# Gated linear attention, soft mixture of experts and gated feed-forward on one core: the first six chunks prepared one at a time, three more w_out blocks converted earlier

## The chip, the cores and the metric

The kernel runs on one core of one Trainium2 chip. The core has five engines that run side by side and meet through semaphores: PE (matrix products, into PSUM), DVE (vector work), ACT (scalar functions and copies), POOL (a second, slower vector engine) and SP, which here only issues DMAs. The metric is the device time of one execution in microseconds (us). Before the change, three runs gave 400.57, 405.32 and 405.67 us; the median is 405.32 us. The profile is of one execution of 403.42 us, whose span from the first to the last instruction is 401.6 us.

## The reference

Three layers follow one another, all in float32 (the gate, value and output weights come as float64):

```python
# attention: 4 batches x 8 heads, 768 tokens, head size 48; the state is 48x48 per head
state = alpha[:, :, t, :, None] * state + einsum('bhd,bhe->bhde', k[:, :, t], v[:, :, t])
y[:, :, t] = einsum('bhd,bhde->bhe', q[:, :, t], state)
# soft mixture of experts: x is 3072 x 384, 8 experts with 4 slots each, hidden 1024
logits = x @ phi
d = softmax over tokens of logits;  c = softmax over slots of logits
slot_out[e] = maximum((d.T @ x)[e] @ w1[e], 0) @ w2[e]
x = c @ slot_out
# gated feed-forward: hidden 1536
xn = x / sqrt(mean(x * x) + 1e-6) * rms_g
out = (silu(xn @ w_gate) * (xn @ w_val)) @ w_out
```

## The kernel before

**Attention.** The 3072 tokens are 24 chunks of 128 tokens, six per batch. A chunk holds all eight heads as four pairs. Within a chunk the recurrence is turned into matrix products: running products of alpha (`R`, L449) and running inverse products from the chunk's other end (`iR`, L457 and L458) scale q and k, then PE makes the scores (L509), ACT moves them out of PSUM (L513), POOL clears what lies after the diagonal (L517), and PE multiplies with v (L530, L535) and with the state carried from the chunk before (L543, L547). DVE writes the next state (L553, op `sv`). The scalings are done for a *unit* of chunks at a time: units of 1, 2 and then 3 chunks, those of 2 and 3 in two halves (two pairs of heads each). One half is: load of alpha, k and q (L431), scans on DVE (L449, L457, L458), k multiplied on DVE and q multiplied on POOL (both L473). Alpha has two buffers, so the third load of alpha waits for the scans of the first.

**The other layers.** After every four chunks the logits, the running softmax over tokens and the slot sums are updated (function `group`). After the last chunk a short chain joins these (L680 to L692) and ends in `siT`, the slots' inputs (op `mi`, L692). The experts follow: 8 products with w1 (L749), each with a relu, a transpose and a product with w2 (L770); w1 and w2 come in 32 loads each (L734, L736) of 384 KB. Then the output side of the mixture is folded into the gate weights (L902 to L928), and the feed-forward runs 72 steps: two products (L1019), silu on ACT (L1054), a multiplication on DVE (L1056), a split into a high part on ACT (L1058) and a low part on DVE (L1061), and twelve products with w_out (L1026 to L1028).

**The float64 weights.** w_gate, w_val and w_out come in 36 pieces of 384 KB. Each is converted by five operations, in the function `wide_ops`: load `cl` (SP, L382), `ca` (ACT, L385 and L386), `cb` (DVE, L389 and L390), `cc` (POOL, L394) and `cd` (DVE, L397). A w_out block is then split into high and low parts (`hi` on ACT, L889, and `lo` mostly on POOL, L891). The first pieces are in the list `sooner`, of length `FIRST`: 15 pieces before the change, that is six gate and value pieces, w_out blocks 0 to 2, and six more gate and value pieces. `HOLD` says what a piece's `ca` waits for: nothing for the first nine, `mi` for those up to `FIRST`, and for pieces 15 to 17 (w_out blocks 3 to 5) `OHOLD`, the first low part of the feed-forward.

**What sets the order.** All operations of the program are entered in a plan with an engine, a cost, a priority, what they follow and which buffers they take. `Plan.times` simulates the engines and puts the operations in an order per engine; the instructions are issued in that order, and each engine and the DMA queue of SP work strictly in it. Besides fixed rings there are 58 blocks (ring `Q`) of 776 columns, of which the attention's buffers cover the first 24 until they are no longer used; weights, conversions and later intermediates take free blocks. A load that has no free block waits at the head of SP's queue, and the loads behind it wait too.

**Warm-up.** `WARM` groups of four transposes of a constant are entered with the lowest priority, so that the plan puts them where it expects PE to idle.

## Time and profile before

| | |
|---|---|
| runs | 400.57, 405.32, 405.67 us |
| profiled execution | 403.42 us, span 401.6 us |
| PE busy | 374.9 us (93%) |
| DVE busy | 299.0 us (74%) |
| ACT busy | 216.8 us (54%) |
| POOL busy | 122.6 us (31%) |
| DMA | 68.43 MB, 48.7% of 16 engines over the span |

The span falls into stages that differ in what limits them, so the shares over the whole span say little. The attention ends at 152.15 us, when the first expert product starts; the experts end at about 183 us; the feed-forward's first product with w_out starts at 194.63 us and the last ends at about 395 us. In a table by stage the columns are the stretch, its length, the busy time and count of each engine's instructions, the granted clock of TensorE (1.00 is 2.4 GHz, 0.50 is 1.2 GHz), the busy share of the 16 DMA engines, and GB/s. In a timeline a row is: start, time taken, engine, line, operation, what it writes and reads, count, and in square brackets the idle time of the engine ahead of it and what ended it.

### The profile page before, as it was taken

The numbers are of one execution on the slowest core, as the hardware profiler recorded it, in microseconds if no ns is written. First come the engines' busy times: TensorE is split into PE (matmuls) and PEld (weight loads), VectorE is DVE, ScalarE is ACT, GpSimd is POOL, SyncE is SP. The second block draws the span as 40 slices with busy tenths as digits, with TensorE's granted clock in tenths as the row PEclk, the third lists the DMA queues.
The fourth block names the chain that finished last, engine by engine and source line by source line (L and its number), as shares of the span: only waits on it lengthen the run. The fifth ranks groups of instructions, "written<-read, shape, count | busy, mean of one in ns | idle before, by whom it ended". The sixth has DMA issues, their size and how long they took to land.

```text
span 401.6 us, 8927 instructions
## 1 busy us (share of the span) xinstructions
PE 374.9 (93%) x3427; PEld 316.1 (79%) x3427; DVE 299.0 (74%) x563; ACT 216.8 (54%) x469; POOL 122.6 (31%) x150
## 2 busy tenths in 40 slices
PE   7689979998899999999889999999999999999993
PEld 6578858785777865436578999979899999999992
DVE  7999979879898557615989987769855667657652
ACT  2336535666574847311676786858856444444440
POOL 3445452635665415600155523243400000000000
PEclk9769989999999999999969999999999999999997
DMA  7899998996989679993021323213000102102012
GB/s 270 282 330 316 333 347 297 341 373 255 341 266 341 204 229 342 346 325 113 2 78 43 116 78 114 85 41 118 0 2 0 53 27 81 55 24 81 32 48 87
DMA packets 29252, 68.43 MB, mean 170 GB/s; under 512 B 3600, under 2 KB 9872, under 8 KB 29200
## 3 DMA queue, kind: packets, MB, share of 16 engines
q1 hardware_dynamic: 29200, 67.77, 48.7%
q8 instruction: 29, 0.48, 0.5%
q14 instruction: 23, 0.19, 0.1%
HBM read 63.04 MB, written 4.72 MB: 169 GB/s over the span
## 4 chain that ended last, share of the span: by engine, by line
PE 64%; DVE 16%; DMA 12%; issue 3%; ACT 2%; POOL 1%; SPq 0%; DVEq 0%; POOLq 0%; ACTq 0%
PE pstr L1019 4%; PE pssc L1019 4%; PE psmisc L1026 3%; PE pskn L1028 3%; PE psmisc L1028 3%; PE psy L1026 3%; PE psmisc L1027 3%; PE psU L1026 3%; PE pssc L509 3%; PE psy L1028 3%; PE psy L1027 3%; PE psU L1028 3%; PE psU L1027 3%; PE pskn L1026 3%; PE psy L530 3%
## 5 line engine op out<-in xcount | busy, mean ns | idle before, releaser
L1061 DVE TENSOR_TENSOR b<-b,b 128x512 fp32r<-128x512 f32 (+1 forms) x73 | 50.7, 697 | 26.3 <-PE psmisc L1027 10.1
L394 POOL TENSOR_TENSOR b<-b 128x384 int32<-128x384 int32 x36 | 40.5, 1126 | 96.5 <-DVE b L390 40.4
L1058 ACT CAST b<-b 128x512 fp32r<-128x512 f32 (+1 forms) x73 | 44.8, 617 | 36.6 <-DVE b L1056 34.5
L1056 DVE TENSOR_TENSOR b<-b,pssc 128x512 f32<-128x512 f32 (+1 forms) x73 | 49.2, 677 | 15.4 <-ACT b L1054 15.0
L1054 ACT ACTIVATE b<-pstr 128x512 f32<-128x512 f32 (+1 forms) x73 | 43.0, 594 | 24.2 <-PE pstr L1019 21.8
L517 POOL TENSOR_SCALAR_AFFINE_SELECT b<-b 128x512 f32<-128x512 f32 x48 | 32.2, 690 | 35.0 <-ACT b L513 34.9
L473 POOL TENSOR_TENSOR b<-b,b 128x768 f32<-128x768 f32 (+1 forms) x17 | 28.9, 1705 | 26.6 <-DVE pstr L457 12.2
L530 PE MATMUL psy<-b,b 128*48 128x128 f32 x384 | 29.7, 295 | 5.2 <-POOL b L517 4.3
L513 ACT COPY b<-pssc 128x512 f32<-128x512 f32 x48 | 26.7, 592 | 12.6 <-PE pssc L509 12.5
L458 DVE TENSOR_TENSOR_SCAN b<-b,pstr 128x387 f32<-128x387 f32 (+1 forms) x34 | 31.0, 912 | 1.7
L449 DVE TENSOR_TENSOR_SCAN b<-b,pstr 128x387 f32<-128x387 f32 (+1 forms) x34 | 29.0, 894 | 3.5 <-DMA b<-in_alpha_rows_dram 3.5
L509 PE MATMUL pssc<-b,b 48*128 48x128 f32 x384 | 30.1, 294 | 1.6 <-ACT b L513 1.2
L397 DVE SCALAR_TENSOR_TENSOR b<-b,b 128x384 int32<-128x384 int32 x36 | 27.2, 764 | 5.8 <-POOL b L394 5.8
L1019 PE MATMUL pssc<-y,b 128*128 128x512 f32 (+1 forms) x73 | 29.3, 401 | 2.1 <-DVE b L1056 1.7
L509 PEld LDWEIGHTS pssc<-b,b 48*128 48x128 f32 x384 | 24.8, 194 | 7.6 <-issue 4.9
L530 PEld LDWEIGHTS psy<-b,b 128*48 128x48 f32 x384 | 22.3, 131 | 10.5 <-POOL b L517 5.2
L1019 PE MATMUL pstr<-y,b 128*128 128x512 f32 (+1 forms) x73 | 29.4, 403 | 0.4 <-DVE b L906 0.4
L385 ACT ACTIVATE b<-b 128x384 f32<-128x384 f32 x36 | 20.8, 577 | 11.6 <-DMA b<-in_moe_w_val_dram 4.1
L1026 PE MATMUL pskn<-b,b 128*128 128x384 f32 x72 | 25.5, 354 | 0.2 <-ACT b L1058 0.2
L1028 PE MATMUL pskn<-b,b 128*128 128x384 f32 x72 | 24.9, 345 | 0.8 <-DVE b L1061 0.8
L1026 PE MATMUL psmisc<-b,b 128*128 128x384 f32 x72 | 24.7, 343 | 0.1
L1026 PE MATMUL psU<-b,b 128*128 128x384 f32 x72 | 24.6, 341 | 0.1
(226 smaller groups left out, 884.0 us busy)
## 6 DMA issues: line engine op xcount, KB each, us to landing
b<-in_moe_w_dram SPq DMA_DIRECT2D x64, 384.0 KB, 5.8
b<-in_alpha_rows_dram SPq DMA_DIRECT2D x14, 387.5 KB, 5.6
b<-in_k_rows_dram SPq DMA_DIRECT2D x14, 384.0 KB, 5.0
b<-in_q_rows_dram SPq DMA_DIRECT2D x14, 384.0 KB, 5.6
b<-in_v_rows_dram SPq DMA_DIRECT2D x24, 192.0 KB, 5.2
b<-in_moe_w_gate_dram SPq DMA_DIRECT2D x12, 384.0 KB, 4.8
b<-in_moe_w_val_dram SPq DMA_DIRECT2D x12, 384.0 KB, 3.9
b<-in_moe_w_out_dram SPq DMA_DIRECT2D x12, 384.0 KB, 3.8
```

What stands on the lines that cost most here:

```text
L394: G.tensor_tensor(ui, ui, r(), ALU.add)
L509: T.matmul(heads(plan(*sc_of(n)[a]))[:, p, :], kq("Tk", n, p)[r], kq("Tq", n, p)[r], start=True, stop=True)
L517: G.affine_select(s, s, pattern=[[0, NP], [1, C]], compare_op=ALU.is_ge, fill=0.0, base=0, channel_multiplier=-1)
L530: T.matmul(y[64 * a:64 * a + D, p, :], vv[:, h], heads(plan("scS", (n, a)))[:, p, :], start=p == 0, stop=first and p == NP - 1)
L1019: T.matmul(plan(r, ("gv", j, f))[:, s], G4(f // 3, a)[:, f % 3 * P:(f % 3 + 1) * P], plan("c4a", j)[:, s].bitcast(F32R), start=True, stop= ...
L1026: T.matmul(po, h, wo_of(f)[:, 0, :], start=(f % HALF == 0), stop=False)
L1027: T.matmul(po, h, wo_of(f)[:, 1, :], start=False, stop=False)
L1028: T.matmul(po, l, wo_of(f)[:, 0, :], start=False, stop=(f % HALF == HALF - 1))
L1054: plan.op(part("sg"), "ACT", 176 + 416 / np, pg, lambda g=g, SG=SG, s=s: A.activation(SG()[:, s], plan(*g)[:, s], AF.Silu), [part("gv"), * ...
L1056: plan.op(part("mu"), "DVE", 130 + 546 / np, pg, lambda val=val, SG=SG, s=s: V.tensor_tensor(SG()[:, s], SG()[:, s], plan(*val)[:, s], ALU ...
L1058: plan.op(part("hh"), "ACT", 194 + 422 / np, pg, lambda SG=SG, HH=HH, s=s: A.copy(HH()[:, s], SG()[:, s]), [part("mu"), *pre("hh")], new=n ...
L1061: lambda SG=SG, HH=HH, HL=HL, s=s: V.tensor_tensor(HL()[:, s], SG()[:, s], HH()[:, s], ALU.subtract), [part("hh"), *pre("hl")], new=new(hl),
```

## The change

Six things change together:

- The units are now six of one chunk and six of three (`SINGLE = 6`), so the first six chunks are scaled one at a time, all pairs at once. Their priorities are their own (`U1`, `U2`), and the state's step `sv` is entered one chunk earlier in priority (`SV = 1`).
- `FIRST` is 18: w_out blocks 3 to 5 join the pieces that wait for `mi` only. `OHOLD` no longer applies to any piece.
- The result of a conversion takes its block when it is written (`cd`), not when its load is issued; a w_out block is written in place, into the block that `ca` takes.
- A constant (`fold`) that DVE made near the start is made on POOL after chunk 4's masks (`folds`).
- `WARM` is 26 instead of 6.
- Some costs and due times of the plan, and the longest wait that it allows an engine for a more urgent operation, are changed.

```diff
-                wait = SOON if x[1] < LATE else WAIT if x[1] < CRIT else LONG
+                wait = SOON if x[1] < LATE else WAIT if x[1] < CRIT else max(LONG, ops[x[3]][1])
...
-BY_POOL = [("q", u) for u in range(9)]
-WARM = 6
+BY_POOL = [("q", u) for u in range(24)]
+WARM = 26
...
-FIRST, PC0, PC_AT, PC_BY, PC_X, PACE = 15, 10, 12, 0.8, 4.5, 1.6
+FIRST, PC0, PC_AT, PC_BY, PC_X, PACE = 18, 10, 12, 0.8, 4.5, 1.6
...
-OHOLD = ("hl", 0, 0)
+OHOLD = ("sT", 1)
...
+U1, U2, SV = -3, 0.8, 1
+SINGLE = 6
...
-EX0, EX_AT, EX_BY = 1, 4, 0.4
-XA, XB, XC, GB1 = 195.8, 197.2, 197.4, 0.5
+EX0, EX_AT, EX_BY = 1, 4, 0.6
+XA, XB, XC, GB1 = 195.8, 198.2, 200.4, 0.5
...
-    u = [(0, 1), (1, 2), (3, 3)] + [(c, 3) for c in range(6, chunks, 3)]
+    u = [(c, 1) for c in range(SINGLE)] + [(c, 3) for c in range(SINGLE, chunks, 3)]
...
-    V.tensor_tensor(fold[:, 0, :], ident[:, 0:32], ident[:, 32:64], ALU.add)
-    V.tensor_tensor(fold[:, 0, :], fold[:, 0, :], ident[:, 64:96], ALU.add)
-    V.tensor_tensor(fold[:, 0, :], fold[:, 0, :], ident[:, 96:128], ALU.add)
-    for g in range(1, 4):
-        V.tensor_copy(fold[:, g, :], fold[:, 0, :])
...
-        plan.op(nm("cl"), "SP", 1130, prio[0], load, after, new=[cv, lim, *new], use=use)
+        plan.op(nm("cl"), "SP", 1190, prio[0], load, after, new=[cv, lim])
...
-        plan.op(nm("cd"), "DVE", 650, prio[1], sign, [nm("cc")], use=[cv, cx, lim, *new, *use])
+        first = [("cd", (*key[:3], 0))] if key[0] == "g" and key[3] else []
+        plan.op(nm("cd"), "DVE", 650, prio[1], sign, [nm("cc"), *first], new=new, use=[cv, cx, lim, *use])
+
+    wf_of = lambda f: ("Q", ("cx", ("o", f)) if wide else ("wf", f))
...
+    def folds():
+        for i in range(1, 4):
+            G.tensor_tensor(fold[:, 0, :], fold[:, 0, :] if i > 1 else ident[:, 0:32], ident[:, 32 * i:32 * i + 32], ALU.add)
+        G.tensor_copy(fold[:, 1:4, :], fold[:, 0:1, :].to_broadcast([P, 3, NS]))
...
-            t = c0 - j + j * g / len(groups) - LD if u else -10
+            t = -10 if not u else U1 + U2 * u if j == 1 else c0 - j + j * g / len(groups) - LD
...
-            plan.op(("sv", n), "DVE", 350, n, lambda n=n: state(n), [("o", n), *[("ck", (u, g)) for g in gs]], use=[("U", n), ("gm", u)])
+            plan.op(("sv", n), "DVE", 350, n - SV, lambda n=n: state(n), [("o", n), *[("ck", (u, g)) for g in gs]], use=[("U", n), ("gm", u)])
...
+    plan.op("fo", "Pool", 900, AHEAD, folds, [("sm", AHEAD, 1)])
```

How instructions move is shown at three places. The lines of the new file are one or a few higher or lower than those above: its L450, L458, L459 and L474 are L449, L457, L458 and L473 of before, and L554 is L553.

The first is DVE near the start, from the multiplication of k that ends the second piece (`b1`). Before:

```order
L473 TENSOR_TENSOR b1_98<-b1_98,b16_113 128x512
L253 TENSOR_TENSOR fold_76<-ident_71 128x32
L254 TENSOR_TENSOR fold_76<-fold_76,ident_71 128x32
L255 TENSOR_TENSOR fold_76<-fold_76,ident_71 128x32
L257 COPY fold_76<-fold_76 128x32 x3
L449 SCALAR_TENSOR_TENSOR b14_111<-b10_107,pstr0_63 128x258 x2
L457 RECIPROCAL pstr1_64<-b14_111 128x2
L458 SCALAR_TENSOR_TENSOR b15_112<-b10_107,pstr1_64 128x258
...
L473 TENSOR_TENSOR b2_99<-b2_99,b15_112 128x512
L449 SCALAR_TENSOR_TENSOR b12_109<-b11_108,pstr0_63 128x387 x2
```

After the change, from the same multiplication:

```order
L474 TENSOR_TENSOR b1_92<-b1_92,b16_107 128x512
L450 SCALAR_TENSOR_TENSOR b14_105<-b10_101,pstr0_63 128x258 x2
L458 RECIPROCAL pstr1_64<-b14_105 128x2
L459 SCALAR_TENSOR_TENSOR b15_106<-b10_101,pstr1_64 128x258
...
L474 TENSOR_TENSOR b2_93<-b2_93,b15_106 128x512
L554 TENSOR_TENSOR b18_109<-psU0_68,b17_108 128x192
L450 SCALAR_TENSOR_TENSOR b12_103<-b11_102,pstr0_63 128x258 x2
```

The constant is gone from here. Before, `b1` and `b2` are the two halves of chunks 1 and 2 and the next piece is half of chunks 3 to 5; now `b1` is chunk 1, `b2` chunk 2, and chunk 3 follows alone, with the first state's step (L554) ahead of it.

The second is SP's queue of DMAs near the end of the experts' weights. Before (L736 loads w2, L382 loads the float64 weights):

```order
L736 DMA b4_2241<-in_moe_w2_dram 128x768
L736 DMA b5_2244<-in_moe_w2_dram 128x768
L382 DMA b2_2256<-in_moe2_w_out_dram 128x768
L382 DMA b7_2260<-in_moe2_w_out_dram 128x768
L382 DMA b9_2271<-in_moe2_w_out_dram 128x768
L382 DMA b14_2419<-in_moe2_w_gate_dram 128x768
```

After (L737 loads w2, L379 the float64 weights):

```order
L737 DMA b32_2141<-in_moe_w2_dram 128x768
L379 DMA b2_2156<-in_moe2_w_val_dram 128x768
L379 DMA b14_2164<-in_moe2_w_out_dram 128x768
L379 DMA b7_2182<-in_moe2_w_out_dram 128x768
L379 DMA b10_2197<-in_moe2_w_out_dram 128x768
L737 DMA b17_2217<-in_moe_w2_dram 128x768
```

Before, the three w_out blocks follow the last load of w2; now the last eleven loads of w2 follow them. From the last load of v to the first load of w2 into a block that held w1 (so that the first expert product must have read it) there are 18 loads before and 26 now; from there to the last load of w2 there are 21 before and 22 now.

The third is DVE where the feed-forward starts. L906 takes the low part of the gate weights, L1056 and L1061 are the feed-forward's multiplication and low part, L389, L390 and L397 convert w_out. Before:

```order
L1061 TENSOR_TENSOR b4_2374<-b12_2360,b3_2371 128x256
L990 SCALAR_TENSOR_TENSOR cN_86<-cN_86,rr_91 128x640
L906 TENSOR_TENSOR b5_2357<-pstr1_64,b5_2357 64x384
L389 TENSOR_SCALAR b12_2390<-b12_2390 128x384
L390 TENSOR_SCALAR b12_2390<-b12_2390 128x384
L906 TENSOR_TENSOR b5_2357<-pssc0_65,b5_2357 64x384
L389 TENSOR_SCALAR b13_2400<-b13_2400 128x384
L390 TENSOR_SCALAR b13_2400<-b13_2400 128x384
L397 SCALAR_TENSOR_TENSOR b6_2257<-b2_2256,b12_2390 128x384
L1056 TENSOR_TENSOR b3_2409<-b3_2409,pssc1_66 128x512
```

After (L907 is L906 of before, L1057 and L1062 are L1056 and L1061, L974 and L975 belong to the norm of the later tokens):

```order
L907 TENSOR_TENSOR b4_2472<-pstr1_64,b4_2472 64x384
L1057 TENSOR_TENSOR b8_2475<-b8_2475,pssc1_66 128x256 x2
L1062 TENSOR_TENSOR b5_2487<-b8_2475,b3_2483 128x256 x2
L907 TENSOR_TENSOR b4_2472<-pssc0_65,b4_2472 64x384
L1057 TENSOR_TENSOR b6_2495<-b6_2495,pssc1_66 128x512
L974 TENSOR_SCALAR rr_85<-ss_84 128x20
L975 TENSOR_SCALAR rr_85<-rr_85 128x20
L1062 TENSOR_TENSOR b12_2520<-b6_2495,b8_2509 128x512
L1057 TENSOR_TENSOR b11_2516<-b11_2516,pssc0_65 128x512
```

The conversions of w_out are gone from between the steps; the three blocks' conversions now stand among the relus and copies of the experts' stage, behind `siT`.

## Rows read from the trace of the kernel before

**Rows 1.** Table by stage of the whole program, columns as named above.
```profile
0.00:28.30 28.30, 21.05 (x168) 17.78 (x168) 25.17 (x50) 8.28 (x22) 12.20 (x22) 0.76 0.85 293
28.30:123.80 95.50, 88.53 (x1388) 73.20 (x1388) 85.13 (x152) 54.94 (x143) 48.17 (x51) 0.98 0.91 320
123.80:152.15 28.35, 26.93 (x387) 20.74 (x383) 17.58 (x46) 17.22 (x44) 11.55 (x13) 1.00 0.75 253
152.15:182.20 30.05, 29.75 (x349) 12.91 (x349) 15.86 (x34) 11.46 (x25) 11.76 (x25) 1.00 0.94 331
182.20:194.60 12.40, 12.29 (x85) 8.63 (x84) 8.69 (x31) 3.82 (x9) 0.00 (x0) 1.00 0.16 61
194.60:201.60 7.00, 4.50 (x20) 2.76 (x18) 6.60 (x16) 4.76 (x10) 2.11 (x2) 1.00 0.00 0
201.60:208.80 7.20, 6.60 (x18) 5.39 (x19) 6.27 (x12) 5.46 (x11) 2.56 (x5) 0.54 0.30 90
208.80:395.00 186.20, 185.26 (x1025) 174.65 (x1023) 133.43 (x226) 110.83 (x207) 34.28 (x34) 1.00 0.17 55
```
**Rows 2.** Timeline of PE in the attention; the last row is the first expert product.
```profile
28.89 1.16 PE L509 MATMUL pssc<-b,b 48*128 48x128 f32 x16
...
48.12 1.08 PE L530 MATMUL psy<-b,b 128*48 128x128 f32 x16
...
55.93 1.73 PE L530 MATMUL psy<-b,b 128*48 128x128 f32 x13 [2.59 <-POOL b L517]
...
152.15 2.80 PE L749 MATMUL pssc<-b,siT 128*32 128x256 f32 x48 [0.35 <-DVE siT L692]
```
**Rows 3.** Groups of DVE's instructions by line and form, first 150 us; mean ns after the comma.
```profile
L458 DVE TENSOR_TENSOR_SCAN b<-b,pstr 128x387 f32<-128x387 f32 x28 | 26.9, 959 | 1.4
L449 DVE TENSOR_TENSOR_SCAN b<-b,pstr 128x387 f32<-128x387 f32 x28 | 25.2, 941 | 2.5 <-DMA b<-in_alpha_rows_dram 2.5
L473 DVE TENSOR_TENSOR b<-b,b 128x768 f32<-128x768 f32 x14 | 14.3, 1022 | 0.3
L389 DVE TENSOR_SCALAR b<-b 128x384 f32<-128x384 f32 x9 | 7.1, 793 | 3.4 <-ACT b L385 3.4
L397 DVE SCALAR_TENSOR_TENSOR b<-b,b 128x384 int32<-128x384 int32 x9 | 7.0, 783 | 0.9 <-POOL b L394 0.9
L457 DVE RECIPROCAL pstr<-b 128x3 f32<-128x3 f32 x28 | 4.9, 175 | 0.5
L458 DVE TENSOR_TENSOR_SCAN b<-b,pstr 128x258 f32<-128x258 f32 x6 | 4.2, 692 | 0.3
L390 DVE TENSOR_SCALAR b<-b 128x384 int32<-128x384 int32 x9 | 3.9, 430 | 0.3
L449 DVE TENSOR_TENSOR_SCAN b<-b,pstr 128x258 f32<-128x258 f32 x6 | 3.8, 674 | 1.1 <-DMA b<-in_alpha_rows_dram 1.1
L473 DVE TENSOR_TENSOR b<-b,b 128x512 f32<-128x512 f32 x3 | 2.6, 867 | 0.1
```
**Rows 4.** Timeline of DVE: first k, the constant, the scan behind it, the last k.
```profile
6.69 1.18 DVE L473 TENSOR_TENSOR b<-b,b 128x512 f32<-128x512 f32 x1
...
11.47 0.61 DVE L253 TENSOR_TENSOR fold<-ident 128x32 f32<-128x32 f32 x1
...
12.84 1.27 DVE L449 TENSOR_TENSOR_SCAN b<-b,pstr 128x258 f32<-128x258 f32 x2
...
122.84 0.95 DVE L473 TENSOR_TENSOR b<-b,b 128x768 f32<-128x768 f32 x1
```
**Rows 5.** Timeline of POOL: first q.
```profile
6.15 1.18 POOL L473 TENSOR_TENSOR b<-b,b 128x512 f32<-128x512 f32 x1 [4.36 <-DMA b<-in_q_rows_dram]
```
**Rows 6.** Timeline of SP's queue: the last thirteen loads of w2.
```profile
161.44 12.88 SPq L736 DMA_DIRECT2D b<-in_moe_w_dram  x13
```
**Rows 7.** Timeline of PE: the end of the experts and the feed-forward's start.
```profile
182.15 0.87 PE L1089 MATMUL psy<-ident 128*128 128x128 f32 x6
...
201.58 0.50 PE L1019 MATMUL pssc<-y,b 128*128 128x512 f32 x1 [1.72 <-DVE b L1056]
```

More of the change, by code (lines that the diff above doesn't have):

```diff
@@ L412, in piece @@
         else:
-            t, w, m, at = ("Q", ("wf", key[1])), wo[key[1] * P:(key[1] + 1) * P], 0, 0
+            t, w, m, at = wf_of(key[1]), wo[key[1] * P:(key[1] + 1) * P], 0, 0
         dst = lambda: plan(*t)[:, at:at + CW]
-        new, use = ([], [t]) if m else ([t], [])
+        new, use = ([], [t]) if m else ([] if wide and key[0] == "o" else [t], [])
         if wide:
@@ L678, in m9 @@
                 T.matmul(plan("kn", "m9")[:, kk * NS:(kk + 1) * NS], acc[:, kk * P:(kk + 1) * P], foldS, start=True, stop=True)
-        plan.op("m1", "PE", 110, prio, lambda: T.transpose(plan("kn", "m1")[0:1, 0:P], m0, ident), [("g1", g)], new=[("kn", "m1")])
+        plan.op("m1", "PE", 110, prio, lambda: T.transpose(plan("kn", "m1")[0:1, 0:P], m0, ident), [("g1", g), *[x for x in ["fo"] if x in plan.ops]], new=[("kn", "m1")])
         plan.op("m2", "DVE", 450, prio, m2, ["m1"], use=[("kn", "m1")])
@@ L739, in experts @@
         for i, x in enumerate(seq):
-            plan.op(("w", *x), "SP", 1130, EX_AT + i * EX_BY, lambda x=x: load(*x), [("w", *seq[i - 1])] if i else after,
+            plan.op(("w", *x), "SP", 1190, EX_AT + i * EX_BY, lambda x=x: load(*x), [("w", *seq[i - 1])] if i else after,
                     new=[("Q", (f"w{x[0]}", *x[1:]))])
@@ L887, in gated @@
                 continue
-            w = ("Q", ("wf", f))
+            w = wf_of(f)
             plan.op(("hi", f), "ACT", 510, po, lambda f=f, w=w: A.copy(wo_of(f)[:, 0, :], plan(*w)[:, 0:DM]), [("cd", key), *(["mi"] if f else [])], new=[("Q", ("wo", f))], use=[w])
@@ L1101, in network @@
             x, w = (u, g), n * j * C
-            t = c0 - j + j * g / len(groups) - LD if u else -10
+            t = -10 if not u else U1 + U2 * u if j == 1 else c0 - j + j * g / len(groups) - LD
             for i, nm in enumerate("akq"):
-                plan.op(("l", nm, x), "SP", 1.45 * w, t - 2 + 0.1 * i, lambda nm=nm, x=x: load_nat(nm, *x), last.get(nm, []), new=[(RING[nm], x)])
+                plan.op(("l", nm, x), "SP", 1.52 * w, t - 2 + 0.1 * i, lambda nm=nm, x=x: load_nat(nm, *x), last.get(nm, []), new=[(RING[nm], x)])
                 last[nm] = [("l", nm, x)]
@@ L1109, in network @@
             for nm in "kq":
-                e, en, cost = (G, "Pool", 2.6 * w) if (nm, u) in BY_POOL else (V, "DVE", 60 + 1.3 * w)
+                e, en, cost = (G, "Pool", 2.35 * w) if (nm, u) in BY_POOL else (V, "DVE", 60 + 1.45 * w)
                 plan.op((nm, x), en, cost, t, lambda nm=nm, x=x, e=e: prep_m(nm, *x, e), [("l", nm, x), ("R" if nm == "q" else "I", x)],
```

## The prediction

> **What bounds the kernel now.** I read the table by stage first, then the timelines of PE and DVE where a stage changes its limit, then the groups of DVE for prices. In the table [rows 1] the reader is to see four things.
>
> From 28.3 to 123.8 us PE is busy 88.53 of 95.50 us and DVE 85.13: both are nearly full, and each waits a little for the other (PE 7.0 us in all, DVE 10.4). DVE's decays come out just ahead of PE's use of them: the last k is done at 122.84 + 0.95 = 123.8 us [rows 4], and 28.4 us later the first expert product starts [rows 2]. In that tail the DMA engines are busy only 0.75 of the time, so 7.1 us of 28.35 are idle.
>
> From 152.15 to 182.20 us the DMA share is 0.94 at 331 GB/s. Thirteen loads of w2 are issued in 12.88 us [rows 6] and PE works through them as they land: this stage hangs on loads.
>
> From 194.6 to 201.6 us PE is busy 4.50 of 7.00 us with DVE at 6.60, and then runs 7.2 us at a granted clock of 0.54, close to its lower level of 1.2 GHz, right after those gaps. PE's longest gap there waits for DVE's L1056 [rows 7], and ahead of that stand the conversions of w_out in DVE's order. The price of this place is 2.5 us idle, 0.6 us idle in the second stretch, and 6.60 x (1 - 0.54) = 3.0 us of slow clock: 6.1 us.
>
> From 208.8 to 395 us PE is busy 185.26 of 186.20 us at full clock. Nothing in the change touches that work, so what counts is when it begins.
>
> The execution took 403.42 us, 1.82 us more than its span; it stands 1.9 us below the median of 405.32.
>
> **The start of the attention.** Single chunks do the same scans in smaller pieces. From the counts in the order, 6 short scans of each direction are added and 4 long ones go: 6 x (0.674 + 0.692) - 4 x (0.941 + 0.959) = +0.6 us; two more reciprocals at 0.175, +0.35; three short k against two long ones, 3 x 0.867 - 2 x 1.022 = +0.6 [rows 3]. The constant leaves DVE, 12.84 - 11.47 = -1.4 us [rows 4]; on POOL its four small instructions stand behind chunk 4's masks, where POOL is busy only 48 of 95.5 us [rows 1], so I cost it at nothing there (if that cover fails, about the same 1.4 us). Ahead of the last k stand three clamps and three sign steps of conversions, instead of five and four: -2 x (0.793 + 0.430) - 0.783 = -3.2 us [rows 3]. Sum on DVE ahead of the last k: 1.55 - 1.4 - 3.2 = **-3.1 us**.
>
> The larger effect is PE's. Before, chunks 3 to 5 can begin only when both halves of their unit are through DVE, and chunk 6's first product with v is at 48.12 us [rows 2]. Now k of chunk 0 is done at 6.69 + 1.18 = 7.9 us [rows 4] and each further chunk costs 2 x 0.674 + 2 x 0.692 + 2 x 0.175 + 0.867 = 3.95 us of DVE, so chunk 5 is ready at 27.6; the two halves of chunks 6 to 8 cost 2 x (2 x 0.941 + 2 x 0.959 + 2 x 0.175 + 1.022) = 10.3 us more, 38 us. PE has then done chunks 0 to 5 and takes chunk 6 at once; with scores, mask and the copies between (I choose 4 us) its product with v is at 42 instead of 48: PE is 6 us ahead. From there it is a race of two nearly full engines. DVE's work alone allows 3.1 us; the 10.4 us that DVE idles are partly waits for PE's states, which come earlier. PE's own 7.0 us of waits, the longest of them 2.59 us on a mask of POOL [rows 2], may shrink. Bounds for the end of the attention: 3.1 (DVE's work only) to 10 us (6 and more than half of PE's idle time) earlier. I take **6 us**, PE's lead with its waits kept.
>
> Weighed against the skill: the first k multiplication took 1.18 us where POOL's q multiplication ran from 6.15 to 7.33 [rows 4, 5], against a mean of 0.867 [rows 3]. The Trainium skill's page "SBUF — State Buffer", section "Who interferes with whom", says that a DVE instruction with two SBUF inputs and a GpSimd instruction that reads SBUF exclude each other for a whole instruction. This row agrees. By that rule taken at each of the six single chunks, 6 x (1.18 - 0.867) = 1.9 us go to such waits and the sum below would be 397.2, inside the forecast's spread; I take the mean, because q of a chunk starts ahead of its k and often ends ahead of it.
>
> **The loads and the experts.** One load of 384 KB takes 393 KB / 331 GB/s = 1.19 us of that stage, 1.12 us of busy DMA at its share of 0.94 [rows 1]. Between the last v and the first w2 that needs a w1 block back there are 26 loads instead of 18: 8 x 1.12 = 9.0 us against 7.1 us of idle DMA, 1.9 us too many. Behind it there are 22 instead of 21 up to the last w2, because the three w_out blocks were put ahead of it: 1.1 us. So the experts end 3.0 us later than they would behind the same `siT`, net **3.0 us earlier** than before. Taking a block only when a result is written frees blocks for these loads; the trace has no row for that, and I bound it by nothing and by the whole 1.9 us.
>
> Three conversions cost DVE 3 x 2.0 us [rows 3]. The order puts them behind `siT`, so not beside the attention but beside the experts, where DVE is busy 15.86 of 30.05 us [rows 1]. I cost them at nothing; should they fall between a relu and its product, up to 6 us of DVE would be on the path. Thirty-six warm-up transposes also stand among the experts, 28 of them ahead of the last product. Six took 0.87 us [rows 7], so 36 are 5.2 us: free while PE waits for w2 (the 3.0 us above), 2.2 us dear otherwise. The other 68 stand ahead of chunk 5's products, where PE waits for DVE.
>
> **The start of the feed-forward.** With the conversions gone, DVE's order goes from the gates' low parts straight to the steps, and the second step's products stand ahead of the first step's products with w_out, so that its silu, multiplication and split run beside 12 products. I take away all but 1 us of the 6.1: **5.1 us**. Bounds: 2.5 us (the idle time of the first stretch alone) to 6.1.
>
> Sum: 3.0 + 5.1 = 8.1 us; 403.42 - 8.1 = **395.3 us**, 10 us or 2.5% below the median.
>
> **The rivals.**
>
> *The loads take the attention's gain.* The experts end with the last w2 whatever DVE and PE do. For it: share 0.94 in that stage, 0.91 ahead of it [rows 1]. Against it: 7.1 us idle in the tail. Only the feed-forward's part stays: 398.3 us.
>
> *The stall moves.* The norm of the later tokens is now split up among the first steps on DVE, and the second group of tokens waits for it; the 5 us turn into 1. For it: DVE at 6.60 of 7.00 us there. Against it: the group is wanted only six steps later, some 15 us at 185.26 / 72 = 2.6 us a step. 399.4 us.
>
> *Slower: blocks, not bandwidth, hold SP's queue.* The place is the queue between the last v and the last w2. If the idle 7.1 us are waits for free blocks that the change keeps, the nine added loads cost 9 x 1.12 = 10.1 us in full. It decides from an attention gain under 10.1 - 5.1 = 5 us on: with only DVE's 3.1 us the time is 403.42 + 10.1 - 5.1 - 3.1 = 405.3, with none 408.4; I take 407. For it: SP works strictly in order, and w1's last loads are now behind more conversions. Against it: a conversion now holds no block for its result while its load is under way.
>
> *Everything comes.* Attention 10 us, experts 1.1 us longer, feed-forward 6.1: 388.4 us.
>
> That the change does not do what it says is partly so: w_out's blocks are not beside the attention. It changes no number, since that cost is at nothing.
>
> **Chances and range.** Forecast 0.60 (spread 390 to 400), loads 0.17, moved stall 0.08, slower 0.07, everything 0.08. From 387.5 to 402.5 us some 0.15 is left out: most of the slower case, part of the best one, tails. About 2% either way, 397.2 and 413.4 us, is what a measurement of this kernel tells from no change. Faster by more: 0.08 from the best case, about 0.43 of the forecast's 0.60, a little of the loads' case: 0.54. Slower by more: 0.03, the tail of that rival. Within: 0.43.
>
> **What would show it.** Attention: the first L749 at about 146 us and chunk 6's first L530 near 42; PE idle from 28 to 118 below 7 us. Loads: DMA share above 0.9 in the attention's tail, experts' end near 179. Feed-forward: first product with w_out near 191.5, granted clock 1.00 from there, no gap of more than 1 us in the first four steps. The forecast is wrong if the first L749 is later than 149, if the experts' stage lasts over 34 us, or if the clock drops again at the feed-forward's start.

## The result, and the profile after

The changed kernel took 390.18 us (median of 4 runs, 389.83 to 391.51) against 404.98 us for the kernel before (4 runs, 400.57 to 405.67): 14.8 us less, a ratio of 0.966 with a 95% interval of 0.959 to 0.974. Medians and ranges in this document are of all executions, while the ratios leave out those in a slower state of the chip, so a ratio is not always the quotient of the two medians beside it. The forecast of 395.3 us was 5.1 us too high, and the time is inside its range. The profiled execution after took 391.51 us with a span of 389.8 us, 11.8 us shorter than the span before. Between the two profiled times lie 11.9 us; the other 2.9 of the 14.8 us are chance, since the profiled execution before lies 1.6 us below its median and the one after 1.3 us above its own.

Engine shares and slices of the page after; in the slices each digit is a busy share, or a clock, in tenths:

```profile
span 389.8 us, 9121 instructions
PE 371.2 (95%) x3507; PEld 317.6 (81%) x3507; DVE 299.1 (77%) x564; ACT 217.6 (56%) x471; POOL 123.3 (32%) x155
...
PEclk9999999999999999989999999999999999999998
```

The low clocks of the first 60 us and of the feed-forward's start are gone; a new, shorter one is in the experts' stage, the 0.95 in the fourth row of the next table. The table by stage after, cut at the last k, the first expert product, the experts' end, the first product with w_out and 20 us behind it, answers to [rows 1]:

```profile
0.00:28.30 28.30, 25.23 (x296) 22.30 (x296) 24.82 (x51) 12.35 (x30) 15.14 (x27) 1.00 0.90 296
28.30:110.50 82.20, 78.05 (x1240) 64.90 (x1240) 77.76 (x144) 48.79 (x132) 43.19 (x49) 1.00 0.97 341
110.50:142.87 32.37, 30.49 (x450) 23.47 (x446) 22.73 (x55) 19.77 (x48) 14.37 (x16) 1.00 0.87 318
142.87:176.65 33.78, 32.05 (x386) 17.43 (x385) 22.19 (x44) 16.51 (x34) 17.16 (x30) 0.95 0.84 296
176.65:189.88 13.23, 13.06 (x91) 9.25 (x87) 9.26 (x30) 4.30 (x11) 0.00 (x0) 1.00 0.00 0
189.88:209.88 20.00, 19.66 (x105) 17.88 (x104) 19.19 (x40) 14.38 (x29) 5.49 (x6) 1.00 0.28 80
```

The timeline of PE after: chunk 6's product with v, the first expert product, two waits for copies of transposed relu results (L764), the experts' warm-ups and last products with w2, the end of the experts, the first product with w_out. It answers to [rows 2, 7]:

```profile
43.49 1.08 PE L531 MATMUL psy<-b,b 128*48 128x128 f32 x16
...
142.87 2.80 PE L750 MATMUL pssc<-b,siT 128*32 128x256 f32 x48
...
166.69 0.33 PE L856 MATMUL pstr<-ident,cN 128*128 128x128 f32 x1 [0.72 <-ACT x L764]
167.91 0.47 PE L856 MATMUL pstr<-ident,cN 128*128 128x128 f32 x1 [0.89 <-DVE x L764]
168.18 1.91 PE L1095 MATMUL psmisc<-ident 128*128 128x128 f32 x8
170.02 2.06 PE L771 MATMUL pskn<-b,x 128*32 128x384 f32 x16
172.01 3.28 PE L1095 MATMUL psmisc<-ident 128*128 128x128 f32 x28
175.22 1.50 PE L771 MATMUL pskn<-b,x 128*32 128x384 f32 x16
176.65 0.87 PE L1095 MATMUL psy<-ident 128*128 128x128 f32 x6
...
189.88 0.34 PE L1027 MATMUL pskn<-b,b 128*128 128x384 f32 x1
```

The timeline of DVE after: the last k, which answers to the last row of [rows 4], then the sign steps (L394) and the low part (L892) of w_out blocks that stand ahead of the second of those copies:

```profile
109.55 0.94 DVE L474 TENSOR_TENSOR b<-b,b 128x768 f32<-128x768 f32 x1
...
163.91 2.32 DVE L394 SCALAR_TENSOR_TENSOR b<-b,b 128x384 int32<-128x384 int32 x3
166.40 1.13 DVE L892 TENSOR_TENSOR b<-b,b 128x384 fp32r<-128x384 f32 x1 [0.16 <-ACT b L890]
167.45 0.41 DVE L764 COPY x<-pstr 128x256 f32<-128x256 f32 x1
```

From these, the 11.8 us between the two spans: the attention ends 152.15 - 142.87 = 9.3 us earlier; the experts' stage lasts 33.8 instead of 182.15 - 152.15 = 30.0 us, 3.8 us longer; what follows lasts 389.8 - 176.65 = 213.15 instead of 401.6 - 182.15 = 219.45 us, 6.3 us less. 9.3 - 3.8 + 6.3 = 11.8. The forecast had 6, 3.0 and 5.1.

### The profile page after: what moved, and what is told of

The parts are those of the page before. It is cut to its first block, busy times and chain, and to the rows that moved or that the text cites. A ratio compares the mean times of both kernels' runs of the same rounds, so it can differ in the third digit from the quotient of the medians.

```text
span 389.8 us, 9121 instructions
## 1 busy us (share of the span) xinstructions
PE 371.2 (95%) x3507; PEld 317.6 (81%) x3507; DVE 299.1 (77%) x564; ACT 217.6 (56%) x471; POOL 123.3 (32%) x155
## 4 chain that ended last, share of the span: by engine, by line
PE 82%; DVE 9%; issue 2%; ACT 2%; DMA 2%; POOL 1%; DVEq 0%; ACTq 0%; POOLq 0%
PE pssc L510 5%; PE psy L531 5%; PE pstr L1020 4%; PE pssc L1020 4%; PE psy L544 4%; PE pskn L1029 3%; PE psy L1027 3%; PE psU L1027 3%; PE psmisc L1027 3%; PE psmisc L1029 3%; PE psy L1028 3%; PE psU L1028 3%; PE psmisc L1028 3%; PE psU L1029 3%; PE psy L1029 3%; PE pskn L1028 3%
## 5 line engine op out<-in xcount | busy, mean ns | idle before, releaser
L1062 DVE TENSOR_TENSOR b<-b,b 128x512 fp32r<-128x512 f32 (+1 forms) x73 | 50.3, 693 | 30.3 <-PE psmisc L1028 11.3
L1057 DVE TENSOR_TENSOR b<-b,pssc 128x512 f32<-128x512 f32 (+1 forms) x73 | 49.0, 675 | 12.7 <-ACT b L1055 12.2
L518 POOL TENSOR_SCALAR_AFFINE_SELECT b<-b 128x512 f32<-128x512 f32 x48 | 33.8, 727 | 28.8 <-ACT b L514 28.8
L474 POOL TENSOR_TENSOR b<-b,b 128x768 f32<-128x768 f32 (+1 forms) x18 | 26.8, 1491 | 20.2 <-DVE pstr L458 12.8
L459 DVE TENSOR_TENSOR_SCAN b<-b,pstr 128x387 f32<-128x387 f32 (+1 forms) x36 | 31.3, 870 | 1.7
L450 DVE TENSOR_TENSOR_SCAN b<-b,pstr 128x387 f32<-128x387 f32 (+1 forms) x36 | 29.2, 849 | 1.3 <-DMA b<-in_alpha_rows_dram 1.3
L510 PE MATMUL pssc<-b,b 48*128 48x128 f32 x384 | 28.3, 285 | 1.7 <-ACT x L564 1.5
L394 DVE SCALAR_TENSOR_TENSOR b<-b,b 128x384 int32<-128x384 int32 x36 | 26.2, 746 | 3.7 <-POOL b L391 3.6
L510 PEld LDWEIGHTS pssc<-b,b 48*128 48x128 f32 x384 | 23.7, 187 | 6.6 <-issue 3.5
L531 PE MATMUL psy<-b,b 128*48 128x128 f32 x384 | 25.9, 277 | 2.3 <-ACT y L1152 1.3
L382 ACT ACTIVATE b<-b 128x384 f32<-128x384 f32 x36 | 21.3, 590 | 12.0 <-DMA b<-in_moe_w_val_dram 5.1
L531 PEld LDWEIGHTS psy<-b,b 128*48 128x48 f32 x384 | 19.9, 122 | 6.4 <-issue 5.0
L1029 PE MATMUL pskn<-b,b 128*128 128x384 f32 x72 | 24.5, 340 | 0.6 <-DVE b L1062 0.6
L1027 PE MATMUL pskn<-b,b 128*128 128x384 f32 x72 | 24.6, 342 | 0.0
L1027 PE MATMUL psy<-b,b 128*128 128x384 f32 x72 | 24.6, 341 | 0.0
```

The lines of the kernel that those rows point to most:

```text
L510: T.matmul(heads(plan(*sc_of(n)[a]))[:, p, :], kq("Tk", n, p)[r], kq("Tq", n, p)[r], start=True, stop=True)
L518: G.affine_select(s, s, pattern=[[0, NP], [1, C]], compare_op=ALU.is_ge, fill=0.0, base=0, channel_multiplier=-1)
L531: T.matmul(y[64 * a:64 * a + D, p, :], vv[:, h], heads(plan("scS", (n, a)))[:, p, :], start=p == 0, stop=first and p == NP - 1)
L1027: T.matmul(po, h, wo_of(f)[:, 0, :], start=(f % HALF == 0), stop=False)
L1029: T.matmul(po, l, wo_of(f)[:, 0, :], start=False, stop=(f % HALF == HALF - 1))
L1057: plan.op(part("mu"), "DVE", 130 + 546 / np, pg, lambda val=val, SG=SG, s=s: V.tensor_tensor(SG()[:, s], SG()[:, s], plan(*val)[:, s], ALU ...
```

## The experiments

Medians stand with the range of the runs; "before" is the median of the kernel before on the same chip (403.95, 403.87 and 403.05 us beside the three groups of four kernels), and ratios are to that kernel. The groups ran on two chips, so a difference of 1 to 2 us between groups says little.

**One part alone, or one part undone.** `b_single`: the kernel before with

```diff
-    u = [(0, 1), (1, 2), (3, 3)] + [(c, 3) for c in range(6, chunks, 3)]
+    u = [(c, 1) for c in range(6)] + [(c, 3) for c in range(6, chunks, 3)]
...
-            t = c0 - j + j * g / len(groups) - LD if u else -10
+            t = -10 if not u else -3 + 0.8 * u if j == 1 else c0 - j + j * g / len(groups) - LD
```

> The kernel before with the first six chunks one at a time and the new due times for them; warm-ups, w_out and the constant as before. My theory: the attention ends 5 to 8 us earlier than at 152.15 and the time is 399 to 401 against 405, because the experts still end with the loads and the feed-forward's stall stays. The rival, that the lead needs the warm-ups' full clock in the first 28 us (0.76 before, 1.00 after): the first expert product is later than 149, time above 402.

404.49 us (401.89 to 405.60), before 403.95, ratio 1.000 (0.996 to 1.004). The run has a flaw of its own: with twelve units, `BY_POOL = range(9)` puts q of the last three on DVE. `b_single2` is the same edit with `range(24)`.

> As b_single, but with q of all units on POOL, as in both the kernel before and the changed one; b_single had left q of the last three units on DVE, six multiplications of about 1 us. My theory (singles give PE 5 us): first expert product at 146 to 148, time 399 to 402. The rival (singles alone give nothing, the lead needs the full clock or the smaller work ahead of the last k): first expert product 150 or later, time above 402.5.

402.95 us (398.45 to 405.96), before 403.87, ratio 0.996 (0.991 to 1.002): no gain that can be measured, first expert product at 152.3 us. In `b_single2` PE stalls near the end of the attention, waiting for loads of v that SP issues only from 116.94 us on; its timeline and its table by stage:

```profile
123.12 1.95 PE L530 MATMUL psy<-b,b 128*48 128x128 f32 x16 [2.76 <-DMA b<-in_v_rows_dram]
```
```profile
116.00:120.00 4.00, 3.99 (x86) 3.21 (x85) 2.05 (x4) 2.83 (x7) 2.19 (x3) 1.00 0.97 328
120.00:132.50 12.50, 9.74 (x90) 8.24 (x83) 10.77 (x20) 4.62 (x13) 5.58 (x5) 0.60 0.67 222
```

In the 12.5 us with the gap and behind it the mean clock is 0.60. `a_units` is the other direction, the changed kernel with the old units:

```diff
-    u = [(c, 1) for c in range(SINGLE)] + [(c, 3) for c in range(SINGLE, chunks, 3)]
+    u = [(0, 1), (1, 2), (3, 3)] + [(c, 3) for c in range(6, chunks, 3)]
```

> The changed kernel with the old units (1, 2, 3 chunks, then threes); all else, the 26 groups of warm-ups too, as changed. In the changed kernel the first expert product is at 142.87 us against 152.15 before. My theory, that the single chunks give PE its lead: chunk 6's first product with v goes back from 43.5 to about 48, the first expert product to 149 to 152, and the time rises by 5 to 8 us to 395 to 398. The rival, that the full clock from the warm-ups or the smaller work ahead of the last k did it: first expert product below 145, time below 392.

392.21 us (391.00 to 395.04), ratio 0.969 (0.961 to 0.977): by the medians 2.0 us above the changed kernel, by the ratios (0.969 and 0.966) not told apart from it. Its profiled execution has the first expert product at 148.0 us, 5.1 later than the changed kernel's, but that execution is its longest (395.04) and has a lower mean clock (0.984) than the three others (0.992 to 0.998), so 2 us is the better size. In its PE timeline chunk 6's product with v comes 3.0 us later than in the changed kernel:

```profile
46.52 1.08 PE L531 MATMUL psy<-b,b 128*48 128x128 f32 x16
```

That lies between the two theories: single chunks give most of the lead at chunk 6 here, but little of the time. My theory that they carry the attention's gain of 9.3 us falls.

**The warm-ups.** `a_warm6` sets `WARM = 6` in the changed kernel, `b_warm26` sets `WARM = 26` in the kernel before.

> The changed kernel with 6 groups of warm-ups instead of 26 (the first 24 transposes stay; those ahead of the products of chunks 0 to 5 and those among the experts are gone). The forecast's reading, that the warm-ups ahead of chunk 5 only fill waits for DVE: attention's end within 1.5 us of 142.9, the experts 2 to 3 us shorter, time 387.5 to 389.5. The rival, that full clock in the first 28 us (0.76 before, 1.00 after) carries the attention's gain: first expert product at 147 or later, time 393 or more.

> The kernel before with 26 groups of warm-ups instead of 6 and nothing else. If the attention's end hangs on DVE there, full clock in the first 28 us changes nothing: 402.5 to 405. If the slow clock there (0.76 of 28.3 us, 6.8 us of PE time at most) was what put PE behind, the first expert product comes 3 to 6 us earlier than at 152.15 and the time is 398 to 401.

`a_warm6`: 398.08 us (393.80 to 399.87), ratio 0.986 (0.981 to 0.991), 7.9 us above the changed kernel, first expert product at 151.3. `b_warm26`: 397.83 us (395.71 to 402.10) against 403.87, ratio 0.987 (0.983 to 0.992), first expert product at 145.5. Here the attention ends 6.7 us earlier without any lead at chunk 6, whose product with v starts at 48.29 us against 48.12 before:

```profile
48.29 1.08 PE L530 MATMUL psy<-b,b 128*48 128x128 f32 x16
```

The forecast priced these groups at nothing ahead of chunk 5; entering them is worth 6 to 8 us. That looked like the clock. `a_keep6` tests it: the changed kernel's order, with all groups behind the sixth left out when the instructions are issued.

```diff
+    given = []
+    def warm_some(bank):
+        given.append(1)
+        if len(given) <= LAST_WARM:
+            warm(bank, 4)
...
-        plan.op(("wu", i), "PE", 436, 1e6, lambda i=i: warm(plan("misc", ("wu", i)), 4), new=[("misc", ("wu", i))])
+        plan.op(("wu", i), "PE", 436, 1e6, lambda i=i: warm_some(plan("misc", ("wu", i))), new=[("misc", ("wu", i))])
```

with `LAST_WARM = 6`.

> The changed kernel in its own order, but of the 26 groups of warm-ups only the first six are issued (24 transposes ahead of the first scores, as in the kernel before); no other instruction is moved. It tells the transposes themselves from the other order that the plan makes without them (a_warm6, 398.1 us). If they work through the granted clock: clock below 1.00 in two or three stretches of the attention again (0.80 to 0.91 in the first 60 us), the last product with v 5 to 9 us later than at 128.8, time 394 to 399, widely spread. If the order did it: within 1.5 us of 388.6, the time without the 28 warm-ups among the experts.

388.99 us (387.91 to 392.41), ratio 0.969 (0.962 to 0.976). `a_keep6` and `a_warm6` issue the same 24 transposes at the start, and 9.1 us lie between them, with intervals of the ratio that do not meet (0.962 to 0.976 and 0.981 to 0.991): the order did it, not the transposes. In its profiled execution (387.93 us) the clock does fall to 0.83 from 10 to 20 us, and this costs nothing that can be seen: chunk 6's product with v starts at 43.53 us, against 43.49 in the changed kernel.

```profile
10.00:20.00 10.00, 8.89 (x124) 7.92 (x124) 8.42 (x17) 4.57 (x15) 6.52 (x8) 0.83 0.98 316
20.00:142.30 122.30, 114.30 (x1773) 92.81 (x1769) 110.94 (x213) 73.29 (x191) 62.25 (x70) 1.00 0.93 332
```
```profile
43.53 1.08 PE L532 MATMUL psy<-b,b 128*48 128x128 f32 x16
```

What the transposes of the attention are worth in other executions is less sure: the four took 387.91, 387.93, 390.05 and 392.41 us, the two longer ones at a mean clock of 0.981 and 0.977 against 0.985 and 0.993.

How an entry that only fills can move the rest: the plan reckons a clock of its own for PE (`pe_time`) and doubles a product's cost where it counts PE as little used. With six groups it doubles six operations of chunks 0 to 2; with 26 none of them. What it believes PE to need late, it puts late on DVE. This is read from the kernel; no run changes the plan's clock alone. The second step of the state (L554), in DVE's timeline of `a_warm6`, stands behind all scans of the next piece:

```profile
25.54 0.69 DVE L459 TENSOR_TENSOR_SCAN b<-b,pstr 128x258 f32<-128x258 f32 x1
26.26 0.17 DVE L458 RECIPROCAL pstr<-b 128x2 f32<-128x2 f32 x1
26.47 0.69 DVE L459 TENSOR_TENSOR_SCAN b<-b,pstr 128x258 f32<-128x258 f32 x1
27.08 0.33 DVE L554 TENSOR_TENSOR b<-psU,b 128x192 f32<-128x192 f32 x1
```

In `a_keep6` (one line number higher) the same second step stands right behind that piece's first scans, 5.6 us earlier:

```profile
20.30 1.26 DVE L451 TENSOR_TENSOR_SCAN b<-b,pstr 128x258 f32<-128x258 f32 x2
21.48 0.33 DVE L555 TENSOR_TENSOR b<-psU,b 128x192 f32<-128x192 f32 x1
```

PE's timeline of `a_warm6` shows who pays, there and again where the slot sums (`acc`) stand on DVE behind the clamps of two conversions:

```profile
27.47 0.88 PE L536 MATMUL psU<-b,b 128*48 128x48 f32 x16 [2.70 <-DVE b L554]
...
121.85 1.11 PE L561 MATMUL psmisc<-ident,y 128*128 128x128 f32 x4 [3.37 <-DVE acc L622]
```

Its table by stage shows the slow clock behind both waits:

```profile
28.30:36.00 7.70, 7.70 (x84) 6.41 (x84) 6.44 (x10) 3.51 (x9) 4.07 (x6) 0.69 0.99 339
...
118.30:128.60 10.30, 6.93 (x60) 6.08 (x59) 7.10 (x12) 4.52 (x10) 7.22 (x9) 0.67 0.89 300
```

By PE's busy time that is an estimated 7.70 x 0.31 + 6.93 x 0.33 = 4.7 us lost to the lower level, beside 2.70 + 3.37 = 6.1 us of waiting. `b_warm14_singles` joins both parts in the kernel before (units, `range(24)`, the state's step at `n - 1`, `WARM = 14`).

> The kernel before with 14 groups of warm-ups, all of them in the attention, the first six chunks one at a time with their new due times, q on POOL, and the state's step one chunk earlier in priority; conversions, w_out and the constant as before. Warm-ups alone gave 6.0 us (397.8), single chunks alone 0.9 us (403.0). If the two add: 396 to 397. If single chunks give their lead only under a full clock: first expert product at 141 to 143 us, time 393 to 395. If they give nothing in either: 397.8.

397.65 us (396.31 to 398.38), before 403.05, ratio 0.987 (0.981 to 0.993): as `b_warm26` alone, with the first expert product at 146.9. PE waits 2.0 us for ACT and 1.7 us for v in its attention. So the single chunks gave nothing there either that these runs can tell.

**The w_out blocks.** `a_wout_late`: the changed kernel with

```diff
-FIRST, PC0, PC_AT, PC_BY, PC_X, PACE = 18, 10, 12, 0.8, 4.5, 1.6
+FIRST, PC0, PC_AT, PC_BY, PC_X, PACE = 15, 10, 12, 0.8, 4.5, 1.6
...
-OHOLD = ("sT", 1)
+OHOLD = ("hl", 0, 0)
```

`a_wout_behind` has the first of the two edits alone: three loads behind w2, conversions behind the experts' last product.

> The changed kernel with w_out blocks 3 to 5 handled as before: loaded behind the last load of w2 and converted from the feed-forward's first low part on. My theory: the experts end about 3.5 us earlier (three loads of 1.19 us less ahead of the last w2), and the feed-forward's start pays 5 to 7 us (gaps of 1 to 2 us for DVE, clock below 1.00 after them), so the time is 391.5 to 394. The rival, that the norm's new place among the steps took the stall away and the conversions cost little there: no slow clock, time 386.5 to 388.5.

> The changed kernel with the loads of w_out blocks 3 to 5 behind the last load of w2 and their conversions behind the experts' last product, not held until the feed-forward's first low part. In the run a_wout_late the experts ended at 169.1 us instead of 176.6 and the stall at the feed-forward's start (gap of 1.95 us, then 0.53 us a product for some 3 us) came back. If conversions at 170 to 190 us find DVE, ACT and POOL free enough: no gap over 1 us, time 384 to 386. If they delay the norm or still stand among the first steps on DVE: 388 to 391.

`a_wout_late`: 390.58 us (389.61 to 393.45), ratio 0.968 (0.959 to 0.977). `a_wout_behind`: 390.56 us (390.18 to 391.60), ratio 0.971 (0.966 to 0.977). Both take as long as the changed kernel. The first row of `a_wout_late`'s table by stage is its experts, the second the feed-forward's start; below it PE's longest gap there:

```profile
141.30:169.10 27.80, 27.64 (x358) 13.62 (x357) 16.00 (x34) 11.75 (x25) 11.70 (x25) 1.00 0.96 341
...
182.60:202.60 20.00, 17.40 (x84) 15.34 (x83) 19.27 (x39) 13.53 (x28) 8.83 (x9) 0.91 0.08 20
```
```profile
191.10 0.50 PE L1020 MATMUL pssc<-y,b 128*128 128x512 f32 x1 [1.95 <-DVE b L1057]
```

The experts are 33.8 - 27.8 = 6.0 us shorter without the three loads, their conversions and the warm-ups ahead of the last w2, and what follows lasts 388.8 - 169.1 = 219.7 us, 6.6 us longer: the move takes with one hand what it gives with the other. In `a_wout_behind` the long gaps are gone (the longest wait is 1.0 us) and the clock is 1.00, yet what follows the experts still lasts 389.8 - 171.3 = 218.5 us, 5.3 us longer than in the changed kernel. Its table by stage behind the first product with w_out, and rows of PE's timeline there:

```profile
184.60:194.60 10.00, 9.25 (x47) 7.68 (x45) 9.75 (x21) 6.59 (x13) 2.43 (x2) 1.00 0.35 118
194.60:204.60 10.00, 9.81 (x60) 8.86 (x60) 9.72 (x25) 6.54 (x13) 5.00 (x6) 1.00 0.06 8
204.60:214.60 10.00, 8.99 (x54) 8.20 (x53) 9.93 (x20) 5.74 (x11) 4.90 (x8) 1.00 0.28 98
```
```profile
201.86 1.09 PE L1095 MATMUL psmisc<-ident 128*128 128x128 f32 x8
203.73 1.91 PE L1095 MATMUL psmisc<-ident 128*128 128x128 f32 x16
206.88 0.50 PE L1020 MATMUL pssc<-y,b 128*128 128x512 f32 x1 [1.01 <-DVE b L1057]
207.82 0.60 PE L1095 MATMUL psmisc<-ident 128*128 128x128 f32 x4
```

PE's busy time there hides lost time: the plan has put 28 warm-up transposes, 3.6 us, between these steps, and the wait of 1.01 us behind the sixteen shows that DVE was late. DVE is then at conversions of gate and value pieces; the last of the three w_out blocks is through its sign step at 191.1 us. Why the feed-forward is longer here is therefore not shown.

**The experts' warm-ups.** `a_nowarm28` is `a_keep6`'s edit with `LAST_WARM = 19`; `a_warm17` sets `WARM = 17`, which leaves those of the attention alone.

> The changed kernel, order untouched, without the 28 warm-up transposes that stand between the last two products with w2 (172.01 to 175.22 us in its trace, while the DMA engines are idle from 172.0 on). If the last w2 block has landed by then, as the traffic says, the experts end about 3.2 us earlier and the time is 387.0. The forecast's reading (the warm-ups fill a wait for w2): no change, 390.2. Third possibility: without them the granted clock falls at the experts' end and takes back 1 to 3 us there: 388 to 390 with a clock below 1.00 from 172 to 190.

> The changed kernel with 17 groups of warm-ups: all those of the attention, none among the experts' products. The run without 28 of the 36 among the experts took 388.6 us against 390.2. If the other eight (168.18 to 170.02 us in the changed kernel's trace) also stand on the path: 387.0 to 388.0. If PE waits there for w2 anyway: 388.6. If the clock needs them: 389.5 or more, with clock below 1.00 behind 165 us.

`a_nowarm28`: 388.62 us (387.34 to 389.42), ratio 0.961 (0.953 to 0.969). By the medians half of the 3.2 us expected came; by the ratios the two kernels are not told apart. Without the transposes the last product with w2 waits for its load, in PE's timeline:

```profile
168.59 2.40 PE L772 MATMUL pskn<-b,x 128*32 128x384 f32 x20
171.33 2.39 PE L772 MATMUL pskn<-b,x 128*32 128x384 f32 x12 [0.34 <-DMA b<-in_moe_w_dram]
```

`a_warm17`: 388.09 us (387.71 to 388.79, 6 runs), ratio 0.964 (0.960 to 0.968). Its median is the lowest of all versions, 2.1 us below the changed kernel's, and all its runs lie below all of that kernel's; but the two were timed apart, and by their ratios to the kernel before (0.964 and 0.966) they are not told apart. Against `a_nowarm28` nothing is told apart either. In its profiled execution (388.79 us) the clock does fall behind 165 us, to 0.50 from 168 to 172, as the third case expected, and the experts' stage lasts 33.1 us, but the time did not rise to 389.5.

**Where a block is taken.** `a_place_load`: the changed kernel with a conversion's block taken when its load is issued (`new=[cv, lim, *new]` at `cl`, none at `cd`) and w_out not written in place.

> The changed kernel with a conversion's result taking its block when the load is issued, as before, and w_out blocks not written in place. In a_wout_late the experts' stage lasted 27.4 us where b_warm26, with the old placing, took 31.4. If the placing is what lets the loads through: first expert product unchanged near 142, the experts' end 2 to 4 us later than at 176.6, time 391.5 to 394. If loads are bound by bandwidth alone: 390 within 1 us.

391.72 us (389.78 to 392.85), ratio 0.974 (0.968 to 0.980): 1.5 us above the changed kernel's median, with ranges that overlap, and its experts end at 175.6 us, not later than 176.6. Inconclusive.

## Why the prediction was right, and where it was not

**The attention's start: the direction right, the mechanism not.** The forecast's "PE is 6 us ahead" at chunk 6, from 48.12 to 42 us, came as 4.6 us (43.49), and the end moved by 9.3 us, near its upper bound of 10. Three steps failed. The first gave the lead to single chunks: alone they give nothing that can be measured (`b_single2`); undone they take 3.0 us of the lead, but only some 2 us of time at the median (`a_units`). The second carried the lead at chunk 6 to the end: in `b_warm26` there is no lead at chunk 6 (48.29), and the end comes 6.7 us earlier all the same. The third costed the warm-ups ahead of chunk 5 at nothing, and the trace before could not show otherwise: the transposes are worth little (`a_keep6` takes 0.4 us more than `a_nowarm28` at the median, not told apart), their entries in the plan 6 to 8 us. What the order bought, by the traces of `a_warm6` and the changed kernel, is that no wait of PE in the attention is long, 1.55 us at most instead of 2.70 and 3.37, and that the clock stays at 2.4 GHz throughout. PE's idle time from 28 to 118 us, 90.0 - 84.4 = 5.6 us, is below the 7 us that I named, but it is no measure of the gain: the forecast said that this time "may shrink", and it shrank from 7.0 by 1.4.

**The slow clock of the first 28 us.** The forecast gave the 0.76 of [rows 1] no term. The profiled execution of `a_keep6` bears that out for 10 to 20 us, at 0.83. Behind waits later in the attention the same clock seems to have cost time, an estimated 4.7 us in `a_warm6`.

**The last k.** The forecast bounded the gain from below by DVE's work ahead of the last k, 3.1 us. The last k is done at 110.49 us instead of 123.79, 13.3 us earlier; behind it stand 32.4 us instead of 28.4, with PE busy 30.49 of 32.37. PE waits for the last k in neither trace: behind 95 us its waits before are for ACT's copies, for POOL and for DVE's slot sums, the longest 1.23 us. So the last k set the end of neither, and the 3.1 us of DVE's work were no lower bound. The six short k took 0.969 us each where I had taken 0.867, 0.6 us more in all.

In this group of DVE after, the second number behind the bar is that mean:

```profile
L474 DVE TENSOR_TENSOR b<-b,b 128x512 f32<-128x512 f32 x6 | 5.8, 969 | 0.2
```

That is not the size of the exclusion, because the mean of 0.867 already holds the first k's 1.18. A k that met no POOL instruction took 0.69 us before; against that the six took 1.65 us more. One of these, the fourth, with the two masks of POOL that were under way, and the k before that met none:

```profile
18.45 1.15 DVE L474 TENSOR_TENSOR b<-b,b 128x512 f32<-128x512 f32 x1
```
```profile
17.84 1.22 POOL L518 TENSOR_SCALAR_AFFINE_SELECT b<-b 128x512 f32<-128x512 f32 x2
```
```profile
15.94 0.69 DVE L473 TENSOR_TENSOR b<-b,b 128x512 f32<-128x512 f32 x1
```

POOL ends at 19.06 us and k at 19.60. Each of the six ends 0.54 to 0.55 us after the end of the POOL instruction under way at its start, of which 0.18 to 0.62 us was left. So the rule that the prediction weighed, from the Trainium skill's page "SBUF — State Buffer", section "Who interferes with whom", by which the two engines exclude each other for a whole instruction, agrees with the trace for k at every one of the six; whether POOL waits in its turn these rows do not settle. The estimate of 1.9 us was off for another reason: it took the first k's wait for all six, and it looked for q, while in five of the six the instruction under way was POOL's mask.

**The experts: 3.0 us forecast, 3.8 measured, and that is luck.** The sum is near because terms of either sign cancel. Three more loads with their conversions cost more than forecast: without the 28 late warm-ups the experts' stage lasts 31.0 us in `a_keep6`, 32.3 in `a_nowarm28` (141.4 to 173.7) and 33.1 in `a_warm17` against 27.8 in `a_wout_late`, so 3.2 to 5.3 us. No run has the loads without the conversions. The conversions were costed at nothing unless they fell between a relu and its product, and there they fell: in the changed kernel DVE does three sign steps and a low part of w_out ahead of a copy that PE needs, and PE waits 0.72 + 0.89 us. `a_keep6`, `a_nowarm28` and `a_warm17` have the same two waits, 1.46 to 1.59 us in all; `a_wout_late`, without the conversions, has none above 0.16. Behind them the clock of the changed kernel is 0.50 from 168 to 170 us, and eight transposes take 1.91 us instead of the 1.04 of `a_nowarm28`. How much of this is on the path is not shown, since PE then waits for the last w2 in all three of those runs. The late warm-ups cost about 1.6 us by the medians, between "free" and the "2.2 dear" that the forecast offered. Against all this the rest of the stage became 2.3 us shorter than before (27.8 against 30.0); which part of the change did that no run separates, since `a_place_load` is inconclusive. The DMA share in the attention's tail was 0.87, not above 0.9, and the stage of 33.8 us stayed just under the 34 at which the forecast called itself wrong.

**The feed-forward's start: the size right.** 6.3 us came where 5.1 were forecast and 6.1 was the bound; clock 1.00, no gap over 1 us. That the conversions of w_out made the stall is shown by `a_wout_late`: with them back, the gap of 1.95 us and the low clock are back. That the gaps and the slow clock make up the price, as the forecast added it up, is not shown: `a_wout_late` takes 6.6 us more behind the experts with them, `a_wout_behind` 5.3 us more with neither. The rival that the norm's new place would bring a new stall did not come.

**What stays open.** In the kernel before, entries and transposes were added together (`b_warm26`), so its 6.0 us are not divided between them. Of the 7.5 us between `b_warm14_singles` and the changed kernel, the w_out blocks explain 0.4 at the median; against `a_wout_late` the rest sits in the attention (first expert product 146.9 against 141.3) and in the experts (30.2 us against 27.8), and is shared by the constant's move, the plan's rule and costs, the number of groups entered and the placing of blocks, which no run takes apart. What is shown is that 6 to 8 of the 14.8 us come with the groups of warm-ups, in the changed kernel through the order, and that the w_out blocks give nothing on balance that can be measured.

The number came nearer than its argument: a lead put down to the wrong part and 3.3 us short at the attention's end, a loss that was sized well by luck, and a gain that was sized well.

## What to carry to other kernels

Where a planner sets the order, a change of a cost, a filler or a priority is a change of the whole order, and its price is read from the order that results; to tell an instruction from its effect on the plan, keep the order and leave the instruction out. Work moved out of a full stage into another is a gain only if that other stage has room on the resource that limits it: here three loads ahead of w2, with their conversions among the experts' products, cost 3.2 to 5.3 us, half or more of the 6.3 that the feed-forward gained. A filler that keeps an engine busy belongs where its end cannot fall behind the data it waits for.

## What the runs showed of the hardware

Executions of one kernel differ more than most of the effects above, and not all kernels alike: 399.99 to 409.17 us for the kernel before, 398.45 to 405.96 for `b_single2`, 393.80 to 399.87 for `a_warm6`, but 389.83 to 391.51 for the changed kernel and 387.71 to 388.79 for `a_warm17`. The wide ones have waits of PE above 2.5 us in the attention and the narrow ones none, yet `a_keep6` has no such wait and spreads from 387.91 to 392.41. Longer executions mostly have the lower mean clock: in `b_warm26` 395.71 us at 0.983 and 402.10 at 0.970. That a wait and the slow clock behind it come in some executions and not in others would fit this; one profile of each cannot show it.

In the first 30 us of the changed kernel DVE's multiplication of k (128x512, two operands) took 0.73 to 1.16 us beside POOL and ended 0.54 to 0.55 us after the POOL instruction that was under way when it started, whether that was q or a mask; a k that met none took 0.69 us in the kernel before. DVE seems to wait there for POOL to finish.
